# Accumulating whole-chunk transfers behind the turned stores, and operand casts behind ScalarE's copies of output blocks

## The chip, the core and the metric

The kernel runs on one core of a Trainium2 chip. The core has a matrix engine (TensorE, PE in the profile; its weight loads are the row PEld), VectorE (DVE), ScalarE (ACT), GpSimd (POOL) and SyncE (SP), each with an instruction queue of its own, worked off in order. Transfers are issued from SP, ACT or POOL and share 16 DMA engines. The metric is the device time of one execution in microseconds (us), the median of several runs.

## What is computed

Three layers follow each other, in fp32: an attention between 8 x 8 sequences and 32 state rows each, and two feed-forward layers.

```
def _moe_ref(x, w_in, w_out):
    h = np.maximum(x @ w_in, 0.0)
    return (h * h @ w_out).astype(np.float32)

def _moe2_ref(x, w1, w2, w3, w_out):          # x: 4352 x 512, w1, w2: 512 x 1024
    a = x @ w1
    b = x @ w2
    h = a * b @ w3                            # w3: 1024 x 1024
    return (h @ w_out).astype(np.float32)     # w_out: 1024 x 512

def reference(**kwargs):
    ...
    attn_out = _attn_ref(**attn_kwargs)       # 8 x 8 x 544 x 64: 512 rows of x, 32 of state
    B, H, S, D = attn_out.shape
    x = np.ascontiguousarray(attn_out.transpose(0, 2, 1, 3)).reshape(B * S, H * D)
    x = _moe_ref(x=x, **moe_kwargs)
    return _moe2_ref(x=x, **moe2_kwargs)
```

The change lies in the last layer, `_moe2_ref`.

## The kernel before

**Rows and passes.** The rows come in nine chunks: eight of 512 rows (one per sequence batch, 0 to 7) and one of 256 rows that holds all state rows. The last layer uses `w3 @ w_out` computed beforehand, so a chunk's result is `(y w1 * y w2) (w3 w_out)`. It goes twice over all chunks: pass `s` = 0 and `s` = 1 each take one half of the 1024 hidden columns, and the results of both are added up. Chunks go in pairs, in pass 0 as (3,4), (5,6), (7,2), (0,1) and in pass 1 in the opposite order.

**fp32 in three matmuls.** Each operand is split into a high part (a cast to fp32r, on ScalarE) and a low part (the difference, on VectorE); three matmuls (`PASSES`) make one product. So wherever an operand is prepared, there is a cast of ScalarE and a subtraction of VectorE behind it.

**Seven products for eight.** A pair of chunks and a pair of column halves form a 2 x 2 block product, which is done with seven block products and a number of sums (block names A11 to A22, B11 to B22; S1 to S4 are sums of A blocks, T1 to T4 sums of B blocks). This is done twice in a pair:

- `quad` (lines 1304 to 1371), four times a pair (m = 0 to 3): from the pair's operands `yq` (made by `make_pair` from the loaded `yraw`) and the weights `wq` come the products of w1 and w2, and `to_z` makes operands `z` of the outcome.
- `out_pair` (lines 1503 to 1651), once a pair: from `z` and the weights `w34b` (or `w`, in pass 0) come the four output blocks 11, 12, 21 and 22. Its products come in the order oa (A11 B11), od (S1 T1), od (S4 B22), oe (A12 B21), oa (S2 T2), oa (S3 T3), oc (A22 T4); `oa`, `od`, `oe` and `oc` are PSUM banks. `keep` copies a half-done block out of PSUM (ScalarE, line 1571), `put` adds the second half (VectorE, line 1578) and stores it. One slot of the weight tile `w34b` holds S4 and S3 in turn; `load_turn` (line 1461) reloads it from DRAM when the product that read it is done.

**Operands of the next pair.** `make_pair` gives eight jobs: B11; a difference; T1; B21; T2; B22; T4; T3. Six of them issue two casts and two subtractions, some of them with two differences ahead. The first two jobs are issued in the pair's fourth quad (`early_jobs`), the rest by `do(n)` in `out_pair`: T1, B21, T2, B22, one at a time, and T4 with T3 at the end. `tc.issue_after(ins)` puts what its block issues behind `ins` on the engine of `ins`; without such an edge a scheduler picks the order on each engine.

**Turned pairs and where their results go.** All pairs but the last of pass 0 and the first and last of pass 1 are "turned" (`turn`): their blocks come out transposed, 32 x 32 pieces are turned back by VectorE in the next pair's quads (`turn_out`, line 1486: blocks 11 and 12 at m = 0, 21 and 22 at m = 1), and stored by eight transfers of 128 KB a chunk, half from SP, half from POOL. In pass 1 the target is not the output but a scratch tensor `osum` per chunk (`half_of` enters it into `to_add`), and `add_turned` later adds each whole chunk to the output by one accumulating transfer from DRAM to DRAM, 1 MB, issued from POOL. In pass 1 this concerns the second pair (7,2) and the third (5,6): two groups of two transfers. Before the change `add_turned` is called in the fourth quad and waits, by a one-column copy of `q1` on POOL (`tick`), for that quad's arithmetic.

**The last pair.** Its kept halves are not copied: pass 0 left the blocks in DRAM (`oscr`), `fetch` loads them as `opart` (line 1560, SP, 256 KB each, two a block) as soon as the buffers are free, and VectorE adds PSUM to them (lines 1567, 1578, 1639). The last product `oc` is stored in four parts as it comes.

Of the kernel before, what the change touches and what calls it, by code (L numbers as in the profile page):

```python
# [13 lines left out]
ALU = mybir.AluOpType  # L14
# [6 lines left out]
def kernel(  # L21
# [17 lines left out]
    nc = tc.nc  # L39
    B, H, S, D = x.shape  # L40
# [4 lines left out]
    T = S + NS  # L45
# [18 lines left out]
    HI, LO = 0, 1  # L64
# [3 lines left out]
    def f32(ap):  # L68
        return ap.bitcast(F32)
# [9 lines left out]
    tick = const.tile([P, 1], F32, name="tick")  # L79
# [10 lines left out]
    def split(hi, lo, src):  # L90
        nc.scalar.copy(hi, src)  # L91
        return nc.vector.tensor_tensor(out=lo, in0=src, in1=f32(hi), op=ALU.subtract)  # L92
# [16 lines left out]
    room, turn, h9 = [att], [], []  # L109
# [562 lines left out]
    last = s1b[1]()  # L672
# [125 lines left out]
    for i, n, src in ((56, 2, A_w["21"]), (62, 2, A_w["22"]), (68, 2, A_w["11"]), (75, 4, s_mem[2]), (82, 4, A_w["12"])):  # L798
        op = {} if i in (56, 75) else {"accum_op": ALU.add}
# [34 lines left out]
    for i, (c, f) in enumerate(order):  # L834
# [7 lines left out]
        gate = done[i - 3] if i >= 8 else first  # L842
# [334 lines left out]
    QM = N1 // 2  # L1177
# [51 lines left out]
    def make_pair(raw):  # L1229

        def put(name, src):
            for kt in range(2):
                tag = SLOT[name][kt]
                t = (bp if tag == "yc" else pa).tile([P, 2, 512], F32R, tag=tag, bufs=BUFS.get(tag, 2), name="yq")
                split(t[:, HI], t[:, LO], src(kt))
                Y[name, kt] = t

        def diff(out, a, b):
            for kt in range(2):
                nc.vector.tensor_tensor(out=out(kt), in0=a(kt), in1=b(kt), op=ALU.subtract)  # L1240

        b11, b12, b21, b22 = ((lambda kt, n=n: raw[kt][:, n]) for n in range(4))
        return [
            lambda: put("B11", b11),
            lambda: diff(b11, b12, b11),
            lambda: put("T1", b11),
            lambda: put("B21", b21),
            lambda: (diff(b11, b22, b11), put("T2", b11)),
            lambda: put("B22", b22),
            lambda: (diff(b21, b21, b11), put("T4", b21)),  # L1250
            lambda: (diff(b12, b22, b12), put("T3", b12)),
        ]

    Z = {}
    left = {}

    def z_tile(slot, name="z"):
        return bp.tile([P, 2, 512], F32R, tag=f"c{slot}", bufs=1, name=name)

    def z_split(slot, name, idx, q):  # L1260
        t = z_tile(slot)
        Z[name, idx] = t
        left["cast"] = nc.scalar.copy(t[:, HI], q)  # L1263
        return nc.vector.tensor_tensor(out=t[:, LO], in0=q, in1=f32(t[:, HI]), op=ALU.subtract)  # L1264

    def minus(t, a, b):
        return nc.vector.tensor_tensor(out=t, in0=a, in1=b, op=ALU.subtract)  # L1267
# [1 line left out]
    def to_z(m, q0, q1):  # L1269

        idx = m // 2
        if m % 2 == 0:
            z_split(1 + idx, "B11", idx, q0)
            minus(q0, q1, q0)
            left["T1", idx], left["B12", idx] = q0, q1
            last = z_split(3 + idx, "T1", idx, q0)
            left["zcast"] = left["cast"]
            return last
        t1, b12 = left.pop(("T1", idx)), left.pop(("B12", idx))
        if idx == 0:  # L1280
            z_split(5, "B22", 0, q1)
        last = minus(t1, q1, t1)
        last = minus(b12, q1, b12)
        left["T2", idx], left["T3", idx] = t1, b12
        if idx == 0:
            z_split(6, "B21", 0, q0)
            last = minus(q0, q0, t1)
            left["T4", 0] = q0
        else:
            left["B22", 1], left["B21", 1] = q1, q0  # L1290
        return last
# [19 lines left out]
    def quad(c0, c1, m, behind, in_order, behind_steps, early_jobs=()):  # L1311
        def product(*args, **kwargs):
            with tc.issue_after(left["quad"].ins) if in_order and "quad" in left else nullcontext():
                left["quad"] = product_of(*args, **kwargs)

        def product_of(ps, w, v, first=True, last=True):
            for kt in range(2):
                for k, (wi, vi) in enumerate(PASSES):
                    mm = nc.tensor.matmul(  # L1319
                        ps, W[w, kt][:, wi, m * P:(m + 1) * P], Y[v, kt][:, vi, :],  # L1320
                        start=(first and kt == 0 and k == 0), stop=(last and kt == 1 and k == 2),
                        skip_group_check=True,
                    )
            return mm

        def kept(i, ps):
            t = bp.tile([P, 512], F32, tag=f"s{i}", bufs=1 + (i == 0), name=f"s{i}")
            left["copy"] = nc.scalar.copy(t, ps)  # L1328
            return t

        def plus(t, ps):
            return nc.vector.tensor_tensor(out=t, in0=ps, in1=t, op=ALU.add)  # L1332

        A, D, E, C = bank_m("qa"), bank_y(m % 2, "qd"), bank_y(2, "qe"), bank_y(3, "qc")
        product(A, "A11", "B11", last=False)
        p1 = kept(0, A)
        with tc.issue_after(behind.ins) if behind else nullcontext():
            product(D, "S1", "T1", last=False)
        p5 = kept(1, D)
        with tc.issue_after(behind.ins) if behind else nullcontext():  # L1340
            product(E, "A12", "B21")
        plus(p1, E)
        product(A, "S2", "T2", first=False, last=False)
        u2 = kept(2, A)
        product(D, "S4", "B22", first=False)
        u2_sum = plus(u2, D)
        with tc.issue_after(u2_sum.ins), tc.issue_after(left["copy"].ins):
            for job in early_jobs:
                job()
        product(C, "A22", "T4")  # L1350
        product(A, "S3", "T3", first=False)
        u3 = kept(3, A)
        plus(p5, A)
        q1 = bp.tile([P, 512], F32, tag="qd" if m % 2 else "qb", bufs=1 if m % 2 else 2, name="q1")
        nc.vector.tensor_tensor(out=q1, in0=u2, in1=p5, op=ALU.mult)  # L1355
        if to_add and m == QM - 1:
            add_turned(q1[:, :1])
        if parts and m in behind_steps:
            add_behind(q1[:, :1])
        if m == 0:  # L1360
            turn_out("11")
        turn_out("21" if m else "12")
        plus(u3, C)
        if m % 2:
            q0 = bp.tile([P, 512], F32, tag="qc", bufs=2, name="q0")
        else:
            q0 = pa.tile([P, 512], F32, tag="r", bufs=2, name="q0")
        nc.vector.tensor_tensor(out=q0, in0=p1, in1=u3, op=ALU.mult)
        if m:
            turn_out("22")  # L1370
        return to_z(m, q0, q1)

    def load9(pool, tag):
# [94 lines left out]
    to_add = {}  # L1468
# [11 lines left out]
    def turn_out(block):  # L1480
        if block not in to_turn:
            return
        rows, ts = to_turn.pop(block)
        o = bp.tile([P, 4 * J, 2, NS], F32, tag=f"c{TURNED[block]}", bufs=1, name="turned")
        for d, t in enumerate(ts):
            nc.vector.transpose(out=o[:, :, d], in_=t)
        dst = rows.rearrange("(k p) (a e) -> a p k e", p=NS, a=4)
        for a in range(4):
            (nc.gpsimd if a % 2 else nc.sync).dma_start(dst[a], o[a * NS:(a + 1) * NS].rearrange("p k d e -> p k (d e)"))

    def add_turned(t):
        gate = nc.gpsimd.tensor_copy(tick, t)
        with tc.issue_after(gate.ins):
            for c in sorted(to_add):
                nc.gpsimd.dma_start(out[c * T:c * T + S, :], to_add.pop(c), accum_op=ALU.add, max_dma_last_dim=512)

    TWO = ("s0", "yo", "r", "qb", "qc")

# [4 lines left out]
    def out_pair(c0, c1, s, jobs, last, first, more):  # L1503
        ends = s == 1 and not more
        turn = more and not (s == 1 and first)
        jobs, gate, zcast = list(jobs), left["copy"], left["zcast"]
        mms = [left["quad"]]

        def do(n):
            with tc.issue_after(last.ins), tc.issue_after(gate.ins), tc.issue_after(zcast.ins):  # L1510
                for job in jobs[:n]:
                    job()
            del jobs[:n]
# [83 lines left out]
        bD = [bank_m("od") for _ in range(2)]  # L1597
        product(bD, "S1", "T1", last=False)
        t22 = keep("22", bD)
        with tc.issue_after(left["kept"].ins) if turn else nullcontext():  # L1600
            do(1 if turn else 3 if more else 2)
        late(1)
        fetch("12")
        product(bD, "S4", "B22", first=False)
# [74 lines left out]
    jobs = make_pair(raw)  # L1679
# [5 lines left out]
    for s, todo in enumerate((turns, turns[::-1])):  # L1685
# [3 lines left out]
        for m in range(QM):  # L1689
            ab9(m)  # L1690
            if s == 0:
                for job in ((1, 2), (3,), (), (4, 5, 6, 7))[m]:
                    gate = left["split9" if m == QM - 1 else "times9"]
# [8 lines left out]
        for i, (c0, c1) in enumerate(todo):  # L1702
            jobs = []
            for m in range(QM):
                early_jobs = []
                if m == QM - 1 and i + 1 < len(todo) and not (s == 1 and i == 0):
                    jobs = make_pair(raw)
                    early_jobs, jobs = jobs[:2], jobs[2:]
                last = quad(c0, c1, m, after if i == 0 else None, i > 1 or s == 0 and (i > 0 or m > 0), (2,) if i else (0, 2), early_jobs)
# [4 lines left out]
            if i + 1 < len(todo):  # L1714
                jobs = jobs or make_pair(raw)
            elif s == 0:
                jobs = make_w(raw)
                jobs[3:4] = [lambda: make9(left.pop("y9")), jobs[3]]
                jobs.insert(2, lambda: left.__setitem__("y9", load9(bp, "qb")))
            more = i + 1 < len(todo)  # L1720
# [34 lines left out]
```

## Time and profile before

| | us |
|---|---|
| median of three runs (1204.85 to 1205.42) | 1204.85 |
| the profiled execution | 1205.78 |
| its span, first to last instruction | 1204.0 |
| busy: TensorE matmul / VectorE / ScalarE / GpSimd | 1186.2 / 958.3 / 693.9 / 176.0 |
| last layer, from the first quad to the last output block: pass 0 / pass 1 | about 713 to 942 / 951 to 1198 |

The median is 0.93 us below the profiled execution; a difference that is worked out from the trace is taken off both. TensorE is busy 99% of the span, so its few gaps are what the time can be shortened by, and VectorE, at 80% over the span, is nearly full in the stretch of the turned pairs.

### The profile page before, as it was taken

To read this page: it belongs to the slowest core of one execution; us is meant where nothing else is said; L and a number is where in the kernel's file an instruction comes from. 1 tells how busy PE (TensorE), PEld (TensorE's weight loads), DVE (VectorE), ACT (ScalarE), POOL (GpSimd) and SP (SyncE) were. 2 spreads that over 40 slices of the span, in tenths; PEclk is the share of its full clock that TensorE was granted. 3 is DMA by queue.
4 is the path that set the end of the run, shared out by engine and by line. 5 is a ranking of instruction groups with operands and counts; after the bars stand their busy time and mean duration, and the time that the engine had idled before them with its cause. 6 is when DMAs were issued, how large, how long until landed. Compare 5 with 4: busy or idle time off the path is not lost.

```text
span 1204.0 us, 18175 instructions
## 1 busy us (share of the span) xinstructions
PE 1186.2 (99%) x6568; PEld 960.0 (80%) x6568; DVE 958.3 (80%) x1713; ACT 693.9 (58%) x1263; POOL 176.0 (15%) x255
## 2 busy tenths in 40 slices
PE   7999999999999999999999999999999999999996
PEld 5677777777777777777888888888888989888786
DVE  7989878778878773677878977989797858698975
ACT  6777556555555565777777654545545436353531
POOL 0000013324231200013220001111010002001111
PEclk9999999999999999999999999999999999999999
DMA  8675768946795923357697686663242814315649
GB/s 251 148 219 194 185 215 227 195 130 176 158 225 159 272 80 109 106 123 114 102 204 245 240 217 107 127 124 108 68 121 74 257 57 77 99 42 133 105 97 201
DMA packets 194994, 183.39 MB, mean 152 GB/s; under 512 B 111944, under 2 KB 147528, under 8 KB 194376
## 3 DMA queue, kind: packets, MB, share of 16 engines
q1 hardware_dynamic: 149576, 111.70, 32.6%
q0 software_dynamic: 43312, 67.12, 26.7%
q10 hardware_dynamic: 2016, 3.41, 0.8%
q8 instruction: 51, 0.84, 0.3%
q14 instruction: 39, 0.32, 0.1%
HBM read 118.62 MB, written 78.25 MB: 164 GB/s over the span
## 4 chain that ended last, share of the span: by engine, by line
PE 94%; DMA 3%; DVE 1%; SPq 1%; ACT 1%; issue 0%; DVEq 0%; ACTq 0%
PE y L594 21%; PE qa L1319 11%; PE qd L1319 7%; PE ps_w L1132 4%; PE qc L1319 4%; PE qe L1319 4%; PE oa L1534 3%; PE qa L966 3%; PE ps_sw L507 3%; PE od L1534 2%; PE ab L1396 2%; PE qd L966 2%; PE oa L1545 2%; PE od L1545 1%; PE y L566 1%; PE oc L1534 1%
## 5 line engine op out<-in xcount | busy, mean ns | idle before, releaser
L594 PE MATMUL y<-ghl,wo 128*128 128x512 f32 x1152 | 280.1, 392 | 0.1
L594 PEld LDWEIGHTS y<-ghl,wo 128*128 128x128 f32 x1152 | 214.4, 188 | 58.0 <-issue 12.6
L1328 ACT COPY s<-qa 128x512 f32<-128x512 f32 x96 | 56.4, 588 | 171.2 <-PE qa L1319 171.2
L1319 PE MATMUL qa<-yq,wq 128*128 128x512 f32 x576 | 142.9, 389 | 0.0
L538 DVE TENSOR_TENSOR ghl<-r,ghl 128x512 fp32r<-128x512 f32 (+1 forms) x112 | 72.5, 647 | 73.0 <-ACT ghl L537 63.8
L1319 PEld LDWEIGHTS qa<-yq,wq 128*128 128x128 f32 x576 | 108.0, 188 | 22.3
L1319 PE MATMUL qd<-yq,wq 128*128 128x512 f32 x384 | 97.4, 389 | 0.0
L1264 DVE TENSOR_TENSOR z<-q,z 128x512 fp32r<-128x512 f32 x112 | 73.4, 682 | 15.9 <-ACT z L1263 15.9
L1319 PEld LDWEIGHTS qd<-yq,wq 128*128 128x128 f32 x384 | 72.1, 188 | 15.0
L1263 ACT CAST z<-q 128x512 fp32r<-128x512 f32 x112 | 67.9, 626 | 26.2 <-DVE q L1355 6.2
L536 ACT ACTIVATE r<-r 128x512 f32<-128x512 f32 (+1 forms) x112 | 67.6, 603 | 4.2 <-DVE yo L605 1.4
L537 ACT CAST ghl<-r 128x512 fp32r<-128x512 f32 (+1 forms) x112 | 66.2, 591 | 2.8
L92 DVE TENSOR_TENSOR yq<-yraw,yq 128x512 fp32r<-128x512 f32 x98 | 64.2, 684 | 3.7 <-ACT yq L91 3.5
L91 ACT CAST yq<-yraw 128x512 fp32r<-128x512 f32 x98 | 57.3, 626 | 5.6 <-DVE yraw L1240 3.5
L1332 DVE TENSOR_TENSOR s<-qa,s 128x512 f32<-128x512 f32 x32 | 22.0, 688 | 43.5 <-ACT s L1328 43.5
L1319 PE MATMUL qc<-yq,wq 128*128 128x512 f32 x192 | 48.7, 389 | 0.0
L1319 PE MATMUL qe<-yq,wq 128*128 128x512 f32 x192 | 48.7, 389 | 0.0
L1132 PE MATMUL ps_w<-wo,w3T 128*128 128x512 f32 x192 | 44.1, 390 | 0.0
L1267 DVE TENSOR_TENSOR q<-q,q 128x512 f32<-128x512 f32 x64 | 43.0, 681 | 0.1
L1319 PEld LDWEIGHTS qc<-yq,wq 128*128 128x128 f32 x192 | 36.0, 188 | 7.5
L1319 PEld LDWEIGHTS qe<-yq,wq 128*128 128x128 f32 x192 | 36.0, 188 | 7.5
L1132 PEld LDWEIGHTS ps_w<-wo,w3T 128*128 128x128 f32 x192 | 35.8, 188 | 7.5
(735 smaller groups left out, 2512.7 us busy)
## 6 DMA issues: line engine op xcount, KB each, us to landing
yraw<-yscr SPq DMA_DIRECT2D x56, 256.0 KB, 5.6
raw<-in_moe_w_out_dram SPq DMA_DIRECT2D x16, 512.0 KB, 4.7
yscr<-yo SPq DMA_DIRECT2D x32, 256.0 KB, 3.7
raw<-in_moe_w_dram POOLq DMA_DIRECT2D x64, 128.0 KB, 3.6
raw<-in_moe_w_dram POOLq DMA_DIRECT2D x16, 512.0 KB, 7.1
raw<-in_moe_w_in_dram SPq DMA_DIRECT2D x12, 512.0 KB, 4.3
xb<-in_x_dram SPq DMA_DIRECT2D x96, 64.0 KB, 3.3
X<-in_x_dram SPq DMA_DIRECT2D x12, 512.0 KB, 8.6
```

The lines of the kernel that those rows point to most:

```text
L91: nc.scalar.copy(hi, src)
L92: return nc.vector.tensor_tensor(out=lo, in0=src, in1=f32(hi), op=ALU.subtract)
L536: nc.scalar.activation(r[:, :n], r[:, :n], ACTF.Square)
L537: casts.append(nc.scalar.copy(t[:, HI, :n], r[:, :n]))
L538: done.append(nc.vector.tensor_tensor(out=t[:, LO, :n], in0=r[:, :n], in1=f32(t[:, HI, :n]), op=ALU.subtract))
L594: mm = nc.tensor.matmul(y_ps[c, d][:, :n], wo_t[f][:, wi, d * P:(d + 1) * P], t[:, gi, :n], start=(f == f0 and k == 0), stop=(f == f1 - 1 ...
L966: nc.tensor.matmul(ps[d], wt[:, wi, d * P:(d + 1) * P], v[:, kt, gi, :], start=(first and kt == 0 and k == 0), stop=(last and kt == 1 and ...
L1132: mm = nc.tensor.matmul(ps, t[:, wi, (j % 4) * P:(j % 4 + 1) * P], wo2_t[j][:, vi, :], start=(j == 0 and k == 0), stop=(j == N1 - 1 and k ...
L1263: left["cast"] = nc.scalar.copy(t[:, HI], q)
L1264: return nc.vector.tensor_tensor(out=t[:, LO], in0=q, in1=f32(t[:, HI]), op=ALU.subtract)
L1319: mm = nc.tensor.matmul(ps, W[w, kt][:, wi, m * P:(m + 1) * P], Y[v, kt][:, vi, :], start=(first and kt == 0 and k == 0), stop=(last and k ...
L1534: mm = nc.tensor.matmul(ps[d], lhs[:, wi, d], Z[v, idx][:, vi, :], start=(first and idx == 0 and k == 0), stop=(last and idx == NB - 1 and ...
```

## The change

Four edits. `add_turned` loses its gate and its one-column copy, and is called right after `turn_out("22")`, that is behind the last turned stores of the chunk, at m = 1 instead of m = 3. In `out_pair` every `do(n)` of a turned pair is issued behind the ScalarE copy that `keep` made last (`left["kept"]`), not only the first; the edge to the cast of T1 in `to_z` (`zcast`) is dropped. The copy `u3` of the fourth quad is issued behind the last cast of the early jobs. `split` is written out in `make_pair` and used in `z_split` (the same instructions).

```
@@ make_pair, z_split, to_z
-                split(t[:, HI], t[:, LO], src(kt))
+                left["yq"] = nc.scalar.copy(t[:, HI], src(kt))
+                nc.vector.tensor_tensor(out=t[:, LO], in0=src(kt), in1=f32(t[:, HI]), op=ALU.subtract)
...
-        left["cast"] = nc.scalar.copy(t[:, HI], q)
-        return nc.vector.tensor_tensor(out=t[:, LO], in0=q, in1=f32(t[:, HI]), op=ALU.subtract)
+        return split(t[:, HI], t[:, LO], q)
...
-            left["zcast"] = left["cast"]
@@ quad
-        u3 = kept(3, A)
+        with tc.issue_after(left["yq"].ins) if early_jobs else nullcontext():
+            u3 = kept(3, A)
...
-        if to_add and m == QM - 1:
-            add_turned(q1[:, :1])
...
         if m:
             turn_out("22")
+            add_turned()
@@ add_turned
-    def add_turned(t):
-        gate = nc.gpsimd.tensor_copy(tick, t)
-        with tc.issue_after(gate.ins):
-            for c in sorted(to_add):
-                nc.gpsimd.dma_start(out[c * T:c * T + S, :], to_add.pop(c), accum_op=ALU.add, max_dma_last_dim=512)
+    def add_turned():
+        for c in sorted(to_add):
+            nc.gpsimd.dma_start(out[c * T:c * T + S, :], to_add.pop(c), accum_op=ALU.add, max_dma_last_dim=512)
@@ out_pair
-        jobs, gate, zcast = list(jobs), left["copy"], left["zcast"]
+        jobs, gate = list(jobs), left["copy"]
...
-            with tc.issue_after(last.ins), tc.issue_after(gate.ins), tc.issue_after(zcast.ins):
+            with tc.issue_after(last.ins), tc.issue_after((left["kept"] if turn else gate).ins):
...
-        with tc.issue_after(left["kept"].ins) if turn else nullcontext():
-            do(1 if turn else 3 if more else 2)
+        do(1 if turn else 3 if more else 2)
```

The end of POOL's queue in pass 1, before: stores of the turned pieces (`osum<-turned`), the copy `tick`, and the accumulating transfers (`out_dram<-osum`) of the third pair.

```order
L1489 DMA osum_11235<-turned 32x16x64 x2
L1489 DMA osum_11268<-turned 32x16x64 x2
L1489 DMA osum_11235<-turned 32x16x64 x2
L1489 DMA osum_11268<-turned 32x16x64 x2
L1492 COPY tick<-q_11621 128x1
L1495 DMA out_dram<-osum_11235 2048x128
L1495 DMA out_dram<-osum_11268 2048x128
```

The same place after:

```order
L1488 DMA osum_11234<-turned 32x16x64 x2
L1488 DMA osum_11267<-turned 32x16x64 x2
L1488 DMA osum_11234<-turned 32x16x64 x2
L1488 DMA osum_11267<-turned 32x16x64 x2
L1492 DMA out_dram<-osum_11234 2048x128
L1492 DMA out_dram<-osum_11267 2048x128
```

Only the copy of the fourth quad's `q1` is gone from between them; the transfers wait for the landing of the stores.

ScalarE in `out_pair` of the third pair of pass 0 (profile time 864 to 881), before: copies of blocks 11 (`o<-oa`) and 22 (`o<-od`), casts of `z`, and casts of the next pair's operands (`yq<-yraw`).

```order
L1571 COPY o<-oa 128x512
L1263 CAST z<-q_8700 128x512
L1571 COPY o<-oa 128x512
L91 CAST yq<-yraw 128x512
L1263 CAST z<-q_8774 128x512
L91 CAST yq<-yraw 128x512
L1263 CAST z<-q_8777 128x512
L1571 COPY o<-od 128x512 x2
L91 CAST yq<-yraw 128x512 x2
```

After:

```order
L1568 COPY o<-oa 128x512
L91 CAST z<-q_8700 128x512
L1568 COPY o<-oa 128x512
L91 CAST z<-q_8774 128x512
L91 CAST z<-q_8777 128x512
L1568 COPY o<-od 128x512 x2
L1235 CAST yq<-yraw 128x512 x2
```

Two operand casts that stood between the copies of 11 and 22 now come later.

The second half of `out_pair` and the start of the next pair's first quad on ScalarE, in the second pair of pass 1 (profile time 1068 to 1080), before: copies of blocks 12 and 21, operand casts, and the quad's copies `s<-qa`, `s<-qd`.

```order
L1571 COPY o<-oa 128x512 x2
L91 CAST yq<-yraw 128x512 x2
L1571 COPY o<-oa 128x512 x2
L1328 COPY s_10826<-qa 128x512
L1328 COPY s_10834<-qd 128x512
L91 CAST yq<-yraw 128x512 x3
```

After:

```order
L1568 COPY o<-oa 128x512 x2
L1235 CAST yq<-yraw 128x512 x4
L1568 COPY o<-oa 128x512 x2
L1327 COPY s_10826<-qa 128x512
L1327 COPY s_10834<-qd 128x512
L1235 CAST yq<-yraw 128x512 x3
```

Four casts instead of two stand between the copies of 12 and of 21; the last casts, behind `s<-qd`, stay where they were.

## Rows read from the trace of the kernel before

**Rows 1.** Waits of PE, 745 to 1204 us: line, releaser, total us, times, longest

```profile
PE oa L1545 <- DMA w34b<-w34u: 3.8, 2, 3.3
PE oa L1534 <- DMA w34b<-w34u: 0.9, 1, 0.9
PE od L1534 <- ACT o L1571: 0.4, 1, 0.4
```

**Rows 2.** Timeline of PE, last pair: start, us, operation, [idle before, releaser]

```profile
1186.09 1.23 PE L1645 MATMUL oc<-w34b,z 128*128 128x256 f32 x9
1190.66 0.59 PE L1545 MATMUL oa<-w34b,z 128*128 128x256 f32 x3 [3.35 <-DMA w34b<-w34u]
1191.72 4.28 PE L1545 MATMUL oa<-w34b,z 128*128 128x256 f32 x21 [0.46 <-DMA w34b<-w34u]
1195.83 1.95 PE L1645 MATMUL oc<-w34b,z 128*128 128x256 f32 x15
```

**Rows 3.** Stretches: length, busy time of engines, granted PE clock, DMA share, GB/s

```profile
1099.00:1118.00 19.00, 19.00 (x85) 15.72 (x84) 14.40 (x24) 8.70 (x17) 1.89 (x3) 1.00 0.00 1
...
1156.00:1165.00 9.00, 9.00 (x41) 7.48 (x40) 6.27 (x11) 2.72 (x5) 0.00 (x0) 1.00 0.01 3
...
1178.00:1199.00 21.00, 15.97 (x116) 15.27 (x115) 12.87 (x22) 2.61 (x5) 1.17 (x1) 0.92 1.26 235
1191.00:1196.00 5.00, 4.54 (x26) 4.33 (x25) 1.07 (x2) 0.00 (x0) 0.00 (x0) 0.66 1.26 246
```

**Rows 4.** Timeline of DVE, last pair, columns as in rows 2

```profile
1176.06 0.68 DVE L1567 TENSOR_TENSOR opart<-oa,opart 128x512 f32<-128x512 f32 x1
...
1187.85 0.69 DVE L1567 TENSOR_TENSOR opart<-oa,opart 128x512 f32<-128x512 f32 x1 [1.45 <-DMA opart<-oscr]
...
1196.64 0.69 DVE L1567 TENSOR_TENSOR opart<-oa,opart 128x512 f32<-128x512 f32 x1 [2.22 <-DMA opart<-oscr]
...
1198.51 1.41 DVE L1639 TENSOR_TENSOR opart<-oc,opart 128x256 f32<-128x256 f32 x4
```

**Rows 5.** DMA issues at 1165-1167, 1120-1122, 1182-1183, 1178-1180: count, KB, us to landing

```profile
opart<-oscr SPq DMA_DIRECT2D x3, 256.0 KB, 2.9
...
w34b<-w34u SPq DMA_DIRECT2D x2, 256.0 KB, 7.1
...
w34b<-w34u SPq DMA_DIRECT2D x2, 256.0 KB, 8.8
...
out_dram<-osum POOLq DMA_DIRECT2D x1, 1024.0 KB, 22.4
```

**Rows 6.** Timeline of POOL in pass 1, columns as in rows 2

```profile
1093.81 1.29 POOL L1489 DMA_DIRECT2D osum<-turned  x2 [1.70 <-DVE turned L1486]
...
1116.71 3.75 POOL L1495 DMA_DIRECT2D out_dram<-osum  x2 [0.45 <-issue]
...
1152.07 1.29 POOL L1489 DMA_DIRECT2D osum<-turned  x2 [1.70 <-DVE turned L1486]
...
1175.43 3.74 POOL L1495 DMA_DIRECT2D out_dram<-osum  x2 [0.45 <-issue]
```

**Rows 7.** Timeline of SP's issues, the loads of block 21

```profile
1185.83 0.97 SPq L1560 DMA_DIRECT2D opart<-oscr  x2
```

**Rows 8.** Timeline of PE, second and third pair of pass 1

```profile
1069.31 2.88 PE L1534 MATMUL oa<-z,w34b 128*128 128x512 f32 x12
...
1127.59 3.40 PE L1534 MATMUL oa<-z,w34b 128*128 128x512 f32 x12 [0.90 <-DMA w34b<-w34u]
```

**Rows 9.** Timeline of ACT, third pair of pass 0

```profile
868.89 0.62 ACT L91 CAST yq<-yraw 128x512 fp32r<-128x512 f32 x1
...
869.94 1.07 ACT L1571 COPY o<-od 128x512 f32<-128x512 f32 x2
```

**Rows 10.** Timelines of DVE and PE, operand T2 in pass 1: made, and read

```profile
1072.72 1.29 DVE L92 TENSOR_TENSOR yq<-yraw,yq 128x512 fp32r<-128x512 f32 x2
...
1078.83 1.52 PE L1319 MATMUL qa<-yq,wq 128*128 128x512 f32 x6
```

## The prediction

> **What bounds the kernel now.** I began with the waits of TensorE over the last third of the run, where the diff works. They are three [rows 1]: 3.8 us for `w34b` in line 1545 (two waits, the longer 3.3), 0.9 us for `w34b` in line 1534, and 0.4 us for ScalarE's copy of an output block. Everything else in that stretch is gapless matmul, so a gain can only come from these three places and from what follows the last of them; what is merely moved on ScalarE, VectorE or a queue beside gapless matmuls is worth nothing.
>
> The last pair's timeline on TensorE [rows 2] shows the first wait at 1190.66, after 3.35 us idle, and a second one of 0.46. The 21 matmuls behind it take 4.28 us. At the pace of the 15 that follow them (1.95 less the 0.28 that the last takes to drain, over 14: 0.119 us each) they would take 2.7: TensorE had fallen idle and then ran partly at the lower of its two clock levels, 1.2 instead of 2.4 GHz; the granted clock of 1191 to 1196 is 0.66 [rows 3].
>
> What VectorE waits for there is a transfer too [rows 4]: the kept part of block 12 comes 1.45 us late (1187.85), that of block 21 2.22 us late (1196.64), and the last four additions end at 1199.92. The run ends 4.1 us later.
>
> Why the transfers are late is read from their times to landing [rows 5]. Three loads of 256 KB issued between 1165 and 1167, with nothing else moving, land in 2.9 us (median). Two of the same size issued between 1182 and 1183 land in 8.8, and two issued between 1120 and 1122 in 7.1. On both occasions POOL had just issued the two accumulating whole-chunk transfers, 1 MB each, at 1175.43 and 1116.71 [rows 6]; the later one of 1175.43's two landed after 22.4 us, thus at about 1199. From 1178 to 1199 the DMA share is 1.26, and it was 0.00 and 0.01 in the 19 us and 9 us that POOL let pass between the turned stores and the accumulating transfers [rows 3].
>
> **The change, part by part.**
>
> *The last two accumulating transfers.* The gate on `q1` of the fourth quad goes, and `tick`'s copy with it (POOL, off every path). POOL's last turned stores are issued at 1152.07 and 1.29 on [rows 6]; the DMA share of 0.01 from 1156 says that all of them had landed by then [rows 3]. The accumulating transfers wait for just that, so they go out at about 1156.5 instead of 1175.43, 19 us earlier. Nothing is queued behind them on POOL but the end of the program, so their wait holds up nobody. How long do they occupy the DMA? At the 235 GB/s of the busy stretch [rows 3] 2.1 MB are 9 us; the slowest row, the 22.4 us, had eight other 256 KB transfers in it. Started at about 1158 they end between 1167 and 1179, both before the loads issued at 1181 to 1186. I take 1174, since about three loads of block parts fall into them.
>
> What the end looks like then: `w34b`, issued just after 1182, lands at the 2.9 us of a quiet queue, near 1185.2, and the second of the two 1.1 us later, which is what 256 KB take at 235 GB/s. The nine `oc` matmuls fill until 1187.2 [rows 2] and the 24 of line 1545 follow without a wait: 2.86, and 15 `oc` 1.8, so TensorE ends at 1191.9 instead of 1197.78. That is 5.9 us: the 3.35 and 0.46 of waiting and some 1.6 of slow clock, and the rest drain. On VectorE block 12's parts are ready when it arrives (1186.4); its four operations of 0.6 us end at 1188.9, and the next one has its matmuls by then. The loads of block 21, issued at 1185.83 and 1186.43 [rows 7], stand behind two stores in SP's queue, most of which is over by then, so I give them 3.7 us and not 2.9: 1189.5 for the first. Three more operations of 0.6 us and the 1.41 of the last four additions [rows 4] make 1192.8 instead of 1199.92, so 7.1 us. TensorE's 5.9 and VectorE's 7.1 meet within a microsecond; VectorE is last and I take 6.8, leaving 0.3 for a bank that comes free late. Bounds: 3.8 if only the idle time goes and the clock and the late loads of block 21 stay, 7.9 if the closing stores, which no longer share, also land 0.8 earlier.
>
> *The first two accumulating transfers.* By the same reading they move from 1116.71 to just behind the stores issued until 1095.1 [rows 6], into 19 us of idle DMA from 1099 to 1118 [rows 3]. The loads issued from 1120 then land in 2.9 and not in 7.1, and `oa` of line 1534 runs as in the pair before, 2.88, instead of 3.40 behind 0.90 of idle [rows 8]: 1.4 us. Bounds: 0.9 (idle alone) and 1.5.
>
> *ScalarE.* The casts of the next pair's operands now stand behind the copies of block 22 (T1, B21) and of block 12 (T2, B22). In the pair at 864 two such casts, the second at 868.89, stand ahead of the two copies at 869.94 [rows 9] for which TensorE waits 0.4 [rows 1]; without the casts the copy is ready about 0.4 earlier, held then by its own product and by the operand cast between. In the other four changed pairs TensorE's list has no such wait, so the copies can be late by a trifle at most. I take 0.7 for the five: 0.4 and four times 0.07. Bounds: 1.4, and a loss of 0.6 if a moved cast costs 0.12 in each pair. Why the casts cost nothing where they went: the operand T2 is finished by 1074.0 in the pair shown and read at 1078.83 [rows 10], and the two casts that are pushed past two copies move by 1.2 us at most. Casts T4 and T3, the ones with little slack, keep their places behind the next quad's copies, as the order shows.
>
> *The rest.* The copy of `u3` behind the early casts stands there already in these pairs. On SP a weight load is issued one store later and another one pair-load earlier, both between the two passes over the chunks, where TensorE shows no wait in the rows; nothing.
>
> Sum: 6.8 + 1.4 + 0.7 = 8.9 us. The profiled execution took 1205.78 with a span of 1204.0, so it would come to 1196.9; the median of the runs, 0.93 lower, to 1204.85 - 8.9 = **1195.9**. The bounds together: 3.8 + 0.9 - 0.6 = 4.1 gives 1200.7, and 7.9 + 1.5 + 1.4 = 10.8 gives 1194.0.
>
> **The rivals.** About 2.4 us (0.2%) either way is what a measurement of this kernel can tell from no change.
>
> *The transfers collide with something else.* The last two now meet the loads of blocks 11 and 22 issued between 1165 and 1167. Those become slower, 7 to 9 us by the rows of shared loads, so they land until about 1175.5; VectorE wants the first at 1176.06 [rows 4]. That is 0.6 us of cover, and where the load takes 3 us more than any of the shared ones TensorE stalls some 2 us in S2 and slows after it: 4 of the 8.9 are gone, 1199.9. For it: the cover is thin. Against: the loads are three, not eight. Chance 0.13.
>
> *The move gives the end nothing.* If the accumulating transfers were through soon after issue, their place would not matter; the late loads would then be due to the loads and stores of 256 KB among themselves, which stay. Only ScalarE's 0.7 would be left: 1204.2. The rows of 22.4 against 2.9 speak against that; what speaks for it is that eight other transfers share those 21 us. Chance 0.07. The Trainium skill has a rule for this case, on the page "DMA: Bandwidth & Descriptors", section "Anatomy of one DMA": a transfer issued by GpSimd takes about 2.0 us plus its bytes over 436 GB/s. By an estimate from that page both would be through 6.8 us after 1175.43, at 1182.2, just when `w34b` is issued, and this rival would hold; the trace has 22.4 and decides against the rule here.
>
> *Slower: the casts arrive too late for the next quad.* Place: the second `qa` product of a pair's first quad, which reads T2. The slack is 4.8 us (1074.0 to 1078.83). If ScalarE's new order, whose four casts now stand between the copies of 12 and 21, held VectorE up by that and d more, five pairs would each lose d and as much again by the slow clock. It decides against the change from 5 x 2d = 8.2 + 2.4, so d = 1.06; with d = 1.5 the time is 1204.85 - 8.2 + 15 = 1211.7. Against: casts are moved by two places of 0.6 us and the slack is four times that. VectorE is busy nearly without a gap in these pairs, so it is not impossible. Chance 0.04.
>
> **How the numbers follow.** Forecast (all three terms, between 1194.0 and 1199) 0.76, collision 0.13, nothing at the end 0.07, slower 0.04. Faster by more than 0.2%: 0.76 and 0.13, so 0.89; same 0.07; slower 0.04. The range leaves out the last two and little of the collision: 1193.9 to 1200.0.
>
> **What would show it.** Right: POOL issues the four transfers near 1099 and 1156; the `w34b` loads near 1120 and 1180 land in about 3 us; both `w34b` waits are gone from TensorE's list; the granted clock stays 1.00 to the last matmul; the copies of block 22 in the pair at 864 come before the casts and the 0.4 falls to 0.1 or so. Wrong: a wait of VectorE in line 1567 for block 11 (collision), loads near 1180 that still take 7 to 9 us although POOL's transfers have landed (nothing gained), or waits of TensorE in line 1319 for `yq` (slower).

## The result and the profile after

The changed kernel takes 1194.83 us (median of 6 runs, 1194.48 to 1196.12), the kernel before, run on the same chip, 1205.17 (6 runs, 1204.85 to 1206.51): a ratio of 0.9915, 95% interval 0.9902 to 0.9928. That is 10.3 us less; 8.9 were forecast (1195.9, range 1193.9 to 1200.0). The profiled execution took 1195.04 us, with a span of 1193.0 against 1204.0 before.

| mark in the trace | before | after | difference |
|---|---|---|---|
| third pair of pass 1, first `oa` to the next quad, us | 20.72 | 19.06 | -1.66 |
| last pair, first `oa` to the last of VectorE's additions | 28.28 | 21.25 | -7.03 |
| end of those additions to the end of the span | 4.07 | 3.10 | -0.97 |
| the four other turned pairs, where only ScalarE's order counts, together | | | -0.70 |
| start of the first pair, where the code is the same | 749.95 | 749.22 | -0.73 |

The first four rows are the change, 10.4 us. The fifth is no part of it: up to that mark the kernels do the same, and in the traces of this case it lies anywhere from 748.2 to 749.95. The stretch from the last pair of pass 0 to the first pair of pass 1 became 0.17 us longer, and with that 10.9 of the span's 11.0 us are accounted for.

TensorE's list of waits from 740 to 1200, which had three rows [rows 1], is empty. Its timeline in the last pair, the three groups that answer to [rows 2] (start, us, operation):

```profile
1183.19 1.25 PE L1641 MATMUL oc<-w34b,z 128*128 128x256 f32 x9
1184.27 3.02 PE L1542 MATMUL oa<-w34b,z 128*128 128x256 f32 x24
1187.13 1.95 PE L1641 MATMUL oc<-w34b,z 128*128 128x256 f32 x15
```

The 24 matmuls that read `w34b` run in one piece, without idle time in front, in 3.02 us; before they were broken into 3 and 21, behind 3.35 and 0.46 of waiting. VectorE, in the places of [rows 4], has no wait for a transfer left:

```profile
1173.14 0.68 DVE L1564 TENSOR_TENSOR opart<-oa,opart 128x512 f32<-128x512 f32 x1
...
1183.43 1.28 DVE L1564 TENSOR_TENSOR opart<-oa,opart 128x512 f32<-128x512 f32 x2
...
1186.52 0.68 DVE L1564 TENSOR_TENSOR opart<-oa,opart 128x512 f32<-128x512 f32 x1
...
1188.54 1.41 DVE L1635 TENSOR_TENSOR opart<-oc,opart 128x256 f32<-128x256 f32 x4
```

POOL's timeline in pass 1, which answers to [rows 6], shows the four moved transfers. The first two go out 5.4 us behind POOL's last turned store, when the stores have landed. Of the last two, the first goes out 1.1 us behind POOL's last turned store and the second 0.8 us behind the first one's issue:

```profile
1092.54 1.29 POOL L1488 DMA_DIRECT2D osum<-turned  x2 [1.70 <-DVE turned L1485]
1099.24 3.75 POOL L1492 DMA_DIRECT2D out_dram<-osum  x2 [5.42 <-DMA osum<-turned]
...
1149.14 1.29 POOL L1488 DMA_DIRECT2D osum<-turned  x2 [1.70 <-DVE turned L1485]
1151.51 1.88 POOL L1492 DMA_DIRECT2D out_dram<-osum  x1 [1.08 <-issue]
1154.23 1.83 POOL L1492 DMA_DIRECT2D out_dram<-osum  x1 [0.84 <-issue]
```

The stretches that answer to [rows 3], with the columns of that group: behind the first two transfers, behind the last two, and the end.

```profile
1099.00:1116.00 17.00, 17.00 (x77) 14.06 (x76) 12.44 (x20) 7.07 (x13) 3.75 (x2) 1.00 1.00 124
1151.00:1171.00 20.00, 20.00 (x99) 16.93 (x98) 13.43 (x23) 6.78 (x12) 3.71 (x2) 1.00 1.04 163
1178.00:1190.00 12.00, 11.08 (x93) 10.87 (x92) 10.64 (x20) 2.28 (x4) 0.00 (x0) 1.00 0.82 267
```

The stretches where the DMA stood idle are now full (share 1.00 and 1.04), with TensorE busy for the whole of both. At the end the granted clock is 1.00, thus 2.4 GHz, up to the last matmul; from 1191 to 1196 of before it was 0.66. Landing times of what is issued from 1099 to 1101, 1119 to 1121, 1151 to 1156, 1162 to 1165 and 1179 to 1180, answering to [rows 5] (count, KB each, median us from issue to landing):

```profile
out_dram<-osum POOLq DMA_DIRECT2D x2, 1024.0 KB, 12.3
...
w34b<-w34u SPq DMA_DIRECT2D x2, 256.0 KB, 3.1
...
out_dram<-osum POOLq DMA_DIRECT2D x2, 1024.0 KB, 13.2
...
opart<-oscr SPq DMA_DIRECT2D x3, 256.0 KB, 6.4
...
w34b<-w34u SPq DMA_DIRECT2D x2, 256.0 KB, 4.5
```

The `w34b` loads of both places are down from 7.1 to 3.1 and from 8.8 to 4.5. The price is in the fourth row: the three loads of block parts, which took 2.9 alone, now run beside the transfers and take 6.4 (6.0 and 6.8; the profile has no landing for the third). Nothing waits for them; that is looked at in the fifth experiment.

### The profile page after: what moved, and what is told of

Read it like the earlier page. It is cut to its first block, busy times and chain, and to the rows that moved or that the text cites. A ratio compares the mean times of both kernels' runs of the same rounds, so it can differ in the third digit from the quotient of the medians.

```text
span 1193.0 us, 18171 instructions
## 1 busy us (share of the span) xinstructions
PE 1182.1 (99%) x6568; PEld 958.4 (80%) x6568; DVE 959.0 (80%) x1713; ACT 695.0 (58%) x1263; POOL 175.1 (15%) x253
## 3 DMA queue, kind: packets, MB, share of 16 engines
q10 hardware_dynamic: 2016, 3.41, 0.8%
## 4 chain that ended last, share of the span: by engine, by line
PE 96%; DMA 2%; SPq 1%; DVE 1%; ACT 0%; issue 0%; DVEq 0%; ACTq 0%
PE y L594 22%; PE qa L1318 11%; PE qd L1318 7%; PE ps_w L1132 4%; PE qe L1318 4%; PE qc L1318 4%; PE oa L1531 3%; PE qa L966 3%; PE ps_sw L507 3%; PE oa L1542 2%; PE od L1531 2%; PE ab L1395 2%; PE qd L966 2%; PE od L1542 1%; PE y L566 1%; PE oc L1531 1%
```

## The experiments

In the first four, the kernel before ran on the same chip at 1204.98 (15 runs); in the last three at 1205.36 (10 runs).

**1. The transfers alone.** Before, with nothing changed but the place of the four accumulating transfers; ScalarE keeps its old order.

```diff
-        if to_add and m == QM - 1:
-            add_turned(q1[:, :1])
...
             turn_out("22")
+            add_turned()
...
-    def add_turned(t):
-        gate = nc.gpsimd.tensor_copy(tick, t)
-        with tc.issue_after(gate.ins):
-            for c in sorted(to_add):
+    def add_turned():
+        for c in sorted(to_add):
```

> Only the accumulating transfers are moved; ScalarE, VectorE, TensorE and SP keep the order of the kernel before. If the transfers are the cause of the end's lateness (my account), this run has all but ScalarE's part: 7.0 at the last pair, 1.0 at the closing stores and 1.7 at the pair before, so 9.7 us less than before, 1195.4, and TensorE's list keeps one wait, for ScalarE's copy in the pair at 864, of 0.4 us. If the new order on ScalarE were what helps (rival), this run would stay at 1205 with both waits for w34b.

Measured: 1195.28, ratio 0.9921 (0.9908 to 0.9935). TensorE's waits in the last third:

```profile
PE od L1531 <- ACT o L1568: 0.5, 1, 0.5
```

Both waits for `w34b` are gone and the one for ScalarE's copy stays, as in the third row of [rows 1]. The transfers alone give nearly all of the gain.

**2. The casts alone.** After, with the transfers put back behind the gate.

```diff
+        if to_add and m == QM - 1:
+            add_turned(q1[:, :1])
...
             turn_out("22")
-            add_turned()
...
-    def add_turned():
-        for c in sorted(to_add):
+    def add_turned(t):
+        gate = nc.gpsimd.tensor_copy(tick, t)
+        with tc.issue_after(gate.ins):
+            for c in sorted(to_add):
```

> The changed kernel with the accumulating transfers put back behind the fourth quad's arithmetic: only the order on ScalarE (and what follows from it on the others) is new. My account: 0.7 us less than before, about 1204.5, too little to be told from no change; the waits for w34b (3.8 and 0.9 us) stand as before, the wait for ScalarE's copy falls under 0.15. Rival (the casts help the end): 1196.

Measured: 1204.98, ratio 0.9999 (0.9991 to 1.0008). The waits:

```profile
PE oa L1545 <- DMA w34b<-w34u: 3.8, 2, 3.3
PE oa L1534 <- DMA w34b<-w34u: 1.5, 2, 1.3
PE od L1534 <- ACT o L1571: 0.2, 1, 0.2
```

The 3.8 is the one of [rows 1], so that wait has nothing to do with the casts. ScalarE's wait fell from 0.4 to 0.2, not under the 0.15 expected, and from the first pair of the stretch to the third pair of pass 1 this profile is 0.56 us shorter than that of before (748.44 to 1110.76 against 749.95 to 1112.83). What was won is lost behind that: the wait in line 1534 is 1.5 instead of 0.9, and the closing stores end 4.94 us behind VectorE's last addition instead of 4.07. The longer wait is not that of a TensorE that comes earlier: within that pair the loads are issued at the same place (7.72 us behind its first `oa`, 7.75 in before) and TensorE needs them at the same place. The loads themselves took longer (7.6 us here, 7.1 in the profile of before). With the transfers in their old place the ScalarE part can't be seen in the time.

**3. Only the last two transfers moved.** The first two stay behind the gate.

```diff
-        if to_add and m == QM - 1:
+        if 7 in to_add and m == QM - 1:
             add_turned(q1[:, :1])
...
             turn_out("22")
+            if 7 not in to_add:
+                add_turned()
...
-    def add_turned(t):
-        gate = nc.gpsimd.tensor_copy(tick, t)
-        with tc.issue_after(gate.ins):
+    def add_turned(t=None):
+        with tc.issue_after(nc.gpsimd.tensor_copy(tick, t).ins) if t is not None else nullcontext():
```

> The kernel before with only the last two accumulating transfers moved; the first two keep their gate. My account: the end's 7.0 and 1.0 us go, the 1.6 of the pair before stay: 8.0 less, about 1197.1, with one wait for w34b of 0.9 us in TensorE's list. If the pair before feeds the end (its delay starts what then collides), much less than 8 would come.

Measured: 1196.78, ratio 0.9934 (0.9922 to 0.9946). The waits:

```profile
PE od L1535 <- ACT o L1572: 0.5, 1, 0.5
PE oa L1535 <- DMA w34b<-w34u: 0.2, 1, 0.2
```

The last pair takes 20.37 us from its first `oa` to TensorE's last matmul (26.15 before, 20.38 after). So the last two transfers alone are worth 8.2 us in the medians, and the first two the 1.5 between this and the first experiment, though the two intervals overlap. The stall that the first two cause varies: 0.2 in this profile, 0.9 in that of before.

**4. The last two transfers left out.** Nothing is moved.

```diff
-                nc.gpsimd.dma_start(out[c * T:c * T + S, :], to_add.pop(c), accum_op=ALU.add, max_dma_last_dim=512)
+                part = to_add.pop(c)
+                if c in (2, 7):
+                    nc.gpsimd.dma_start(out[c * T:c * T + S, :], part, accum_op=ALU.add, max_dma_last_dim=512)
```

> The kernel before with the last two accumulating transfers left out altogether (chunks 5 and 6 lack the second pass's part), the first two where they were. If the moved transfers cost nothing where they now run (my account), this comes to the same time as the run that moves them alone, about 1197.1, within 0.5 us. If they still cost something there (they slow the loads of blocks 11 and 22), this is faster by that, 1 to 2 us. If the loads and stores of the end are late by themselves (the rival of the prediction), it stays at 1204 to 1205.

Measured: 1197.46, ratio 0.994 (0.9928 to 0.9952), 0.7 us above the third experiment where at most 0.5 was expected; the two intervals overlap. In the profiles a difference of 0.71 lies in the pair before, 20.69 us against 19.98, where the first two transfers stand in their old place in both. TensorE in the last pair:

```profile
1185.29 1.24 PE L1647 MATMUL oc<-w34b,z 128*128 128x256 f32 x9
1186.36 3.03 PE L1547 MATMUL oa<-w34b,z 128*128 128x256 f32 x24
1189.23 1.95 PE L1647 MATMUL oc<-w34b,z 128*128 128x256 f32 x15
```

Without the transfers the pair takes 20.34 us, with them moved 20.37. Where they now run they cost nothing in these profiles, and what they cost before came from running beside the loads of the end. Whether the two share the DMA engines or the memory behind them, no run separates. The rival by which the loads hinder each other, without the transfers, falls.

**5. The transfers part of the way back.** After, with the gate put back, but on the third quad (m = 2) and not on the fourth.

```diff
+        if to_add and m == 2:
+            add_turned(q1[:, :1])
...
             turn_out("22")
-            add_turned()
...
-    def add_turned():
-        for c in sorted(to_add):
+    def add_turned(t):
+        gate = nc.gpsimd.tensor_copy(tick, t)
+        with tc.issue_after(gate.ins):
+            for c in sorted(to_add):
```

> The changed kernel with the accumulating transfers gated on the third quad's product q1 instead of following the last turned stores: they start about 12 us later, near 1163 and 1106, half-way to where they were before. Two lone transfers of this kind take 15 us from issue to landing in the changed kernel's trace (1099.2 to 1114.9), so the last pair's would end near 1180, just under the w34b loads of 1179, and share with the loads of blocks 11 and 22. My account (what counts is the overlap with the loads of w34b and of block 21): a little of the end is lost, 1 to 2 us, 1196 to 1197. Rival (any place ahead of the fourth quad's end does): 1194.8. Rival (the loads of blocks 11 and 22 come late and stall TensorE, the collision of the prediction): a wait in line 1564 for block 11 and 1198 or more.

Measured: 1200.77, ratio 0.9967 (0.9954 to 0.9979), so 6 us slower than after. My account said 1196 to 1197; the rival of a collision was right. The first two transfers, issued at 1105.4, are not the cause: the third pair takes 19.07 us, as in after. TensorE's waits:

```profile
PE oa L1545 <- DVE opart L1567: 3.4, 1, 3.4
```

TensorE's timeline in the last pair:

```profile
1178.54 0.58 PE L1545 MATMUL oa<-s,z 128*128 128x256 f32 x1 [3.35 <-DVE opart L1567]
1179.14 1.65 PE L1545 MATMUL oe<-w34b,z 128*128 128x256 f32 x6
1180.59 4.60 PE L1545 MATMUL od<-w34b,z 128*128 128x256 f32 x24
```

VectorE's timeline there:

```profile
1177.80 0.69 DVE L1567 TENSOR_TENSOR opart<-oa,opart 128x512 f32<-128x512 f32 x1 [3.83 <-DMA opart<-oscr]
```

The landing of what was issued from 1162 to 1165:

```profile
out_dram<-osum POOLq DMA_DIRECT2D x2, 1024.0 KB, 14.3
opart<-oscr SPq DMA_DIRECT2D x3, 256.0 KB, 2.8
```

VectorE waits 3.83 us for a block part, TensorE 3.35 for the bank that this addition frees, and the 24 matmuls that follow take 4.60 instead of 3.02, at a granted clock of 0.58 (stretch of this kernel, columns of [rows 3]):

```profile
1180.00:1185.00 5.00, 5.00 (x28) 5.00 (x28) 2.09 (x4) 0.13 (x1) 0.00 (x0) 0.58 0.34 110
```

The transfers were issued at 1162.5, with three block loads beside them that landed in 2.8. So it is not those loads that come late. The late one is the next, the second half of block 11. SP's timeline of before shows its issue:

```profile
1174.37 0.36 SPq L1560 DMA_DIRECT2D opart<-oscr  x1
```

SP's timeline of after:

```profile
1171.44 0.36 SPq L1557 DMA_DIRECT2D opart<-oscr  x1
```

SP's timeline of this kernel:

```profile
1170.99 0.36 SPq L1560 DMA_DIRECT2D opart<-oscr  x1
```

Its reader starts at 1177.26 in before, at 1174.36 in after and at 1177.80 here. From issue to use it has 2.9 us where nothing disturbs it, which is what such a load takes alone [rows 5]: next to no cover. Here it needed 6.8, beside transfers that were issued from 1162.5 and took a median of 14.3. In after the last transfer, issued at 1154.23, landed 15.4 us later (DMA issues of after from 1154 to 1156):

```profile
out_dram<-osum POOLq DMA_DIRECT2D x1, 1024.0 KB, 15.4
```

That is 1169.6, or 1.8 us before this load is issued. The last two transfers fit between the turned stores and this load, with 1.8 us to spare in this profile. The first, third and sixth experiments have them in the same place, and their profiles show how much this varies: the last transfer took 13.0, 12.5 and 12.0 us, and 4.2, 4.8 and 3.9 us were left before the load was issued.

**6. The casts later still.** After, with all the early casts of the next pair's operands behind ScalarE's copies of block 12, in the turned pairs.

```diff
-        do(1 if turn else 3 if more else 2)
+        if not turn:
+            do(3 if more else 2)
...
-        do(1)
+        if not turn:
+            do(1)
...
-        do(1)
+        if not turn:
+            do(1)
...
         put("12", t12, bD)
-        do(1)
+        do(4 if turn else 1)
```

> The changed kernel with the four operand jobs T1, B21, T2 and B22 of a turned pair all issued behind ScalarE's copies of block 12, so that T1 and B21 come some 7 us later: a larger dose of the move that the change makes on ScalarE. If T2's 4.8 us is the slack that counts (as I put it in the prediction), nothing happens: the last casts of the eight are over before the quad reads them, 1194.8. If VectorE counts, which is full from here to the next quad and has its last subtraction (T3) only 0.3 us ahead of the matmul that reads it, four subtractions of 0.6 us that no longer run earlier arrive as lateness: 1 to 2 us in each of five pairs, 1200 to 1205, with waits of TensorE in line 1318 for yq.

Measured: 1201.58, ratio 0.997 (0.9958 to 0.9981), 6.7 us slower than after. TensorE's waits:

```profile
PE qe L1318 <- DVE o L1575: 5.8, 5, 1.2
```

One of the five places, on TensorE's timeline:

```profile
1080.93 1.62 PE L1318 MATMUL qe<-yq,wq 128*128 128x512 f32 x6 [1.15 <-DVE o L1575]
```

And on VectorE's:

```profile
1076.49 2.50 DVE L1236 TENSOR_TENSOR yq<-yraw,yq 128x512 fp32r<-128x512 f32 x4
1078.89 1.29 DVE L1575 TENSOR_TENSOR o<-oa,o 128x512 f32<-128x512 f32 x2
1080.09 1.29 DVE L1575 TENSOR_TENSOR o<-oc,o 128x512 f32<-128x512 f32 x2
```

Four of the five turned pairs are 1.4 us longer (first `oa` of one to first `oa` of the next 58.52 us against 57.12, at the first pair), and the third of pass 0 is 0.9 us longer (58.53 against 57.61). But TensorE doesn't wait for an operand: the last low part of the early casts is done at 1078.99, and the second `qa` product that my slack was about would have begun 4.1 us behind the first (1076.89), at 1081.0. It waits for VectorE's addition of block 21, whose first half frees the bank that the next quad's `qe` takes. The addition in after, on VectorE's timeline:

```profile
1074.11 1.28 DVE L1575 TENSOR_TENSOR o<-oc,o 128x512 f32<-128x512 f32 x2
```

And the `qe` product of after, on TensorE's:

```profile
1076.20 1.52 PE L1318 MATMUL qe<-yq,wq 128*128 128x512 f32 x6
```

There the first half of the addition ends near 1074.8 (1.28 us for two, one of them 0.68), 1.4 us before `qe`. The two pairs start 3.41 us apart (1054.44 in after, 1057.85 here), so the addition is 2.57 us later within its pair; less the 1.4 that is 1.17, and the wait is 1.15. With the casts late, VectorE's low parts of these operands, which stand ahead of the addition in its order, come late with them, and VectorE has no gap there to catch up in.

**7. One of the last two transfers left out.** As the fourth, with `if c != 6`.

```diff
+                part = to_add.pop(c)
+                if c != 6:
+                    nc.gpsimd.dma_start(out[c * T:c * T + S, :], part, accum_op=ALU.add, max_dma_last_dim=512)
```

> The kernel before with one of the last two accumulating transfers left out (chunk 6 lacks the second pass's part), the other in its place. If the end is late by sharing the DMA with them, half of them gives an end in between: the one left lands about 10 us after 1175.4, thus near 1186, the w34b loads of 1182 land in 5 to 6 us instead of 8.8, and block 21's loads are free again: 1198 to 1200. If only the last-landing transfer counted (an all-or-nothing wait), 1197 or 1205.

Measured: 1198.63, ratio 0.9943 (0.9929 to 0.9957), within the 1198 to 1200 expected. Landing of the transfer that is left (issued from 1173 to 1177), of the loads behind it (1180 to 1183), and of the first of these alone (1180 to 1180.5):

```profile
out_dram<-osum POOLq DMA_DIRECT2D x1, 1024.0 KB, 10.1
...
w34b<-w34u SPq DMA_DIRECT2D x2, 256.0 KB, 6.2
...
w34b<-w34u SPq DMA_DIRECT2D x1, 256.0 KB, 6.1
```

TensorE's wait in the last pair:

```profile
PE oa L1547 <- DVE opart L1569: 1.0, 1, 1.0
```

With two, one and none of the transfers at the end, `w34b` lands in 8.8, 6.2 and 4.2 us (the last from the fourth experiment), and the last pair takes 26.15, 21.79 and 20.34 us. Halving the bytes takes away three quarters of the pair's loss, not half. The lateness of the loads falls about evenly, but TensorE loses only what reaches beyond the matmuls in front, and behind this wait of 1.0 us the granted clock stays at 1.00 (1186 to 1190), where it was 0.66 behind the 3.35 of before. The list puts the wait down to an addition of VectorE, which ended at 1186.53 and had itself waited for loads of block 12; the first `w34b` load, issued at 1180.35, landed 6.1 us later, near 1186.45, so `w34b` alone would have held TensorE nearly as long. The times can't tell this run from the fourth, as their intervals overlap: the step from one transfer to none is read from one profile of each.

## Why the prediction was right, point by point

**The mechanism.** That the accumulating transfers make the loads of the end late is shown: moved (first and third experiment) or left out (fourth), both waits for `w34b` in line 1545 go, and with one left (seventh) only 1.0 us of waiting remains there. The casts alone leave it as it was (second).

**The last pair: forecast 6.8, measured 7.0, and 1.0 for the closing stores.** TensorE's 5.9 came out as 5.77, VectorE's 7.1 as 7.03. The step "they would take 2.7" for the 21 matmuls at full clock held: all 24 took 3.02, and the clock stayed at 1.00. One value in between was off: `w34b` landed in 4.5 and not in 2.9 (with no transfers at all it was 4.2, so it is the stores and loads of the end themselves that make it slower), and the `oc` matmuls in front covered that. The closing stores were taken at 0 with 0.8 as a bound; end of additions to end of span fell by 0.97, a little more than the bound, and that is most of what the forecast lacks.

**The pair before: forecast 1.4, measured 1.66.** The profile of before had 0.90 of idle there, and 12 matmuls that took 0.52 longer. That was not the clock, which is 1.00 from 1127.5 to 1131, but for the most part the second load: it lands when three of the 12 have run. The chain of work that ended last, in before (start, us, what):

```profile
1121.28 7.31 DMA w34b<-w34u
...
1128.64 2.35 PE oa L1534 x9
```

In the first experiment, without ScalarE's part, the pair takes 19.15, which leaves 1.57 for the transfers; the other 0.09 is ScalarE's. This term moves from run to run: with the first two transfers in their old place the pair takes 20.72 us in before and 21.17, 19.98, 20.69 and 20.84 in the second, third, fourth and seventh experiment.

**ScalarE: forecast 0.7 for five pairs, measured 0.70 in the lengths of four** (0.13, 0.08 and 0.35 in pass 0, 0.13 in the second pair of pass 1), and the 0.09 above in the fifth. Between after and the first experiment, which differ in that part alone, the five pairs differ by 0.71. The times of the two kernels, 1194.83 and 1195.28, are too close to show it. The rows are as forecast: in the third pair of pass 0 the copies of block 22 come before the early casts, and TensorE's idle time falls from 0.45 to 0.13 us, as forecast; the pair is still 0.5 us longer than the first one, 19.53 against 19.04. ScalarE's timeline of after:

```profile
868.68 1.12 ACT L1568 COPY o<-od 128x512 f32<-128x512 f32 x2
869.70 1.15 ACT L1235 CAST yq<-yraw 128x512 fp32r<-128x512 f32 x2
```

TensorE's timeline there:

```profile
866.23 2.95 PE L1531 MATMUL od<-z,s 128*128 128x512 f32 x12
869.31 3.00 PE L1531 MATMUL od<-z,w 128*128 128x512 f32 x12
```

**How long the transfers occupy the DMA: right by luck.** The estimate was 9 us for 2.1 MB at the 235 GB/s of the end, started at 1158 and ended by 1174. They were issued at 1151.51 and 1154.23 (the forecast 1156.5 is 1153.6 in the time of after, whose last pair starts 2.93 us earlier) and were through at 1169.6, thus 18 us. The first two, with nothing else moving, landed 10.0 us (the first) and in the median 12.3 us behind their issues at 1099.24 and about 1.1 later, so the second needed 14.6 and both together 15.7. The issues from 1099 to 1100 of after:

```profile
out_dram<-osum POOLq DMA_DIRECT2D x1, 1024.0 KB, 10.0
```

The rate of a stretch that mixes these transfers with loads isn't theirs. The estimate let them end as late as 1179; the load of block 11 that has next to no cover is issued at 1174.37 in the time of before, so within that estimate lay a loss that the sum did not have. The margin in front of that load came out as 1.8 to 4.8 us in four profiles.

**The rivals.** *The move gives nothing at the end* is refuted by the third and fourth experiments; the 15.7 us of the first two in their quiet stretch speak against it by themselves. The rule of the Trainium skill ("DMA: Bandwidth & Descriptors", "Anatomy of one DMA"), from which 6.8 us for both were estimated, does not hold for these transfers. *The collision* named a real danger at the wrong load. The loads issued between 1165 and 1167 of before, now between 1162 and 1165, did become slower, 6.4 us for 2.9 in the median, a little under the 7 to 9; and the first of them is issued at 1162.53 and used at 1173.14, so that nothing came near to using up its cover. The load with next to no cover is the one issued at 1171.44, which the prediction did not look at, and the fifth experiment shows what it costs when hit: 6 us. *Slower* put its decision on the wrong resource. The step was "The slack is 4.8 us (1074.0 to 1078.83)", the slack of operand T2. In the sixth experiment that slack was not used up, and the pairs became 0.9 to 1.4 us longer all the same, by way of VectorE and the bank of block 21, whose slack is 1.4 us. The rival's other doubt, that VectorE is busy nearly without a gap, was the one that decides, and its price of "as much again by the slow clock" was not seen: 1.15 us of wait in a loss of 1.4 us per pair, at a granted clock of 1.00 (1079 to 1084).

**What stays open.** Whether the margin between the transfers' end and the load of block 11, 1.8 to 4.8 us in four profiles, is ever used up: the six runs of after lie within 1.7 us, which leaves no room for a loss of 6. And what exactly the transfers and the loads share.

## What to carry to other kernels

A bulk transfer off the critical path is placed by what else is moving while it lasts, not by when its result is wanted: look for a stretch where the DMA share is near 0, and measure the transfer's own duration in a quiet place before deciding that it fits. The slack of a small load is the time from its issue to its use less what it takes alone; list that for every load in the stretch into which a transfer moves, for the one that has none stalls the pair. When work is pushed back on one engine, the slack that counts may belong to a buffer that a full engine behind it frees, and not to the data that was pushed.

## What the runs showed of the hardware

Accumulating transfers from DRAM to DRAM are slow even alone: 2.1 MB in 15.7 us with nothing else moving (and again in the fifth experiment's profile, 1105.38 to 1121.1, beside two loads at the end), with a DMA share of 1.00 and 124 GB/s in that stretch, while the stretch of mixed loads and stores at the end of after has 267 GB/s with a share of 0.82.

A stall on TensorE can cost nearly twice its length: behind the idle 3.35 us of the fifth experiment the granted clock was 0.58 from 1180 to 1185, thus for the most part at the lower of its two levels, 1.2 GHz, 24 matmuls took 4.60 us instead of 3.02, and the last pair took 26.47 us up to TensorE's last matmul instead of 20.38, 6.1 more. The shorter stalls of these runs did not have that price: behind the 1.15 us of the sixth the granted clock stayed at 1.00, and the first six matmuls took 1.62 us; the same six take 1.52 in the pairs' other three quads, where they don't wait.
